# First batch: the tails of q and k are cast by GpSimd, without warming matmuls ahead of their transposes, and one h1 block is evacuated by ScalarE

## The chip, the cores and the metric

The kernel runs on one core of a Trainium2 chip. The time is device microseconds of one execution. Three executions of the kernel before gave 298.59, 298.76 and 299.44 us; the median is 298.76 us. One more execution was recorded by the hardware profiler; all rows of a trace come from that one.

The engines are named as the profile names them: PE is the tensor engine (PEld its weight loads), DVE the vector engine, ACT the scalar engine, POOL is GpSimd, and SP only issues transfers. Each runs its own queue in order and waits on semaphores for the others.

## The reference, cut to what matters

Two layers, one after the other. First an attention over 8 batches, 8 heads, 576 positions and 64 columns a head, in which heads 0 to 3 ("plain") see the last 32 positions and heads 4 to 7 ("dilated") every fourth of the last 128:

```python
scores = scale * np.matmul(q, k.transpose(0, 1, 3, 2))
mask_plain = (rel >= 0) & (rel < 32)
mask_dil = (rel >= 0) & (rel < 128) & (rel % 4 == 0)
attn = softmax(np.where(masks, scores, -1e9))
x = np.matmul(attn, v)            # to (batch, 576, 512): heads beside each other
```

Then a mixer on `x`, first over the positions, then over the columns:

```python
h = np.maximum(xt @ w_tok1, 0.0) @ w_tok2      # 576 -> 256 -> 576, xt is x transposed
u = x + h.transpose(0, 2, 1)
h2 = np.maximum(u @ w_ch1, 0.0) @ w_ch2        # 512 -> 1536 -> 512
return u + h2
```

Inputs and output are float32; the kernel computes in float16 with float32 sums.

## The kernel before, in words

**Tiles.** Positions are worked on in blocks of 128: four full blocks and a tail of 64 (positions 512 to 575). For q and k the 512 main positions of a pair of heads (hp = 0 to 3) lie in `l_q` and `l_k` in float32 and are cast to float16 (`c_q`, `c_k`; `cast_qk`, L252). The tails of q and k of all heads lie together in one tile `lt`, q in partitions 0 to 63 and k in 64 to 127; one cast (`cast_tails_qk`, L258, recorded at the helper's line L103) makes `c_t` of it.

**From cast to scores.** PE transposes the casts into PSUM (`transposes`, L304, tiles `tp_q` and `tp_k`). For the first batch ACT or DVE copies q into `qz` and DVE copies k into `kt` (L315). The tails have a function of their own in the first batch, `first_tails` (L388): four transposes of `c_t` into `tp_t`, and three copies on DVE into `qz` (L398, twice) and `kt` (L399). Scores (`sc` and, for the last blocks, `sm`) are matmuls of `kt` and `qz` (L406) with a masking matmul ahead of each (L404); ACT takes the exponential into `attp` (plain) or `attd` (dilated). `values` (L471) multiplies with v into `av`; DVE forms a reciprocal (L501) and the normalised `xn`.

**The mixer.** `emit_h1` (L504) makes h1 in four pieces: `jb` counts the two blocks of 128 hidden rows, and `half` the two halves of the columns, 0 for the plain heads and 1 for the dilated. Each piece is five matmuls into `h1p` and one relu on its way to SBUF. In the first batch `u_half` (L819) then makes u piece by piece. `w1n` is the first token weight with its rows in natural order; `natural_w1` (L779) builds it on PE from `w1p` and `spread`. `emit_uT` transposes u, and the channel matmuls (`gp`, L645, then `yp`, L664) follow.

**The order.** It is written out by hand: each engine executes its instructions in the order in which the program emits them. The first batch is a straight list (L717 to L850); after it a generator of channel matmuls for batch b is interleaved with steps of the batches behind it, by planned times. POOL's list for the first batch runs L743 to L765: a cast of q, the late memsets (`emit_fixed_late`, L171), then transfers of weights and casts of q, k and v in turn. POOL issues those weight transfers itself, so they stand in the same order as its casts; SP and ACT issue the loads of q, k and v. The second batch's loads start behind two small copies on POOL (`gate`, L732) that wait for weight transfers.

**PSUM.** Three banks called `fl` and three called `main` are taken in turn, and two for scores. `warm` (L708) takes a `main` bank and runs matmuls of zeros (`idle`) into it that nobody reads: eight at the start (L767) and two at L794.

The list of the first batch around the change:

```python
    tp(1)
    cast_tails_qk(0, nc.vector)
    warm(2)
    first_tails()
    ts[7]()
    ts[8]()
    cast_qk(0, "k", 2, nc.vector)
    ts[10]()
```

Here `tp(hp)` is the transposes of q and k of a pair of heads with their copies, and `ts[5 * hp + i]` is step i of that pair: 0 and 1 the transposes of q and k, 2 and 3 the scores of its two heads, 4 the last blocks.

Of the kernel before, what the change touches and what calls it, by code (L numbers as in the profile page):

```python
# [69 lines left out]
def kernel(  # L70
# [11 lines left out]
    nc = tc.nc  # L82
# [9 lines left out]
    def bank(tag, bufs, name, dtype=FP32):  # L92

        if tag in turn:
            turn[tag] += 1
            tag, bufs = f"{tag}{turn[tag] % bufs}", 1
        return ps.tile([128, 512 if dtype == FP32 else 1024], dtype, tag=tag, bufs=bufs, name=name)

    def copy(eng, out, in_):
        if eng is nc.scalar:  # L100
            nc.scalar.copy(out=out, in_=in_)  # L101
        else:
            eng.tensor_copy(out=out, in_=in_)  # L103

    def relu(eng, out, in_):
        if eng is nc.scalar:
            nc.scalar.activation(out=out, in_=in_, func=AF.Relu)  # L107
        else:
            eng.tensor_scalar_max(out=out, in0=in_, scalar1=0.0)  # L109
# [61 lines left out]
    def emit_fixed_late():  # L171
        for i in range(2):
            nc.gpsimd.memset(vv[i][64:128, 4], 0.0)
            nc.gpsimd.memset(vv[i][:, :, :, 64:65], 1.0)
            nc.gpsimd.memset(vt[i][:, :, 64:65], 1.0)
            nc.gpsimd.memset(w1t[i], 0.0)
        nc.gpsimd.memset(w2a[:, :, S:640], 0.0)
# [74 lines left out]
    def cast_qk(b, nm, hp, eng):  # L252
        if (b, nm) not in c16:
            c16[(b, nm)] = sb.tile([128, 4, 4, 2, D], FP16, tag=f"c_{nm}", bufs=1, name=f"c_{nm}_{b}")
        copy(eng, c16[(b, nm)][:, hp],
             l32[(b, nm, hp // 2)][:, 2 * (hp % 2):2 * (hp % 2) + 2].rearrange("m h r d -> m r h d"))

    def cast_tails_qk(b, eng):  # L258
        c16[(b, "t")] = sb.tile([128, H, D], FP16, tag="c_t", bufs=1, name=f"c_t_{b}")
        copy(eng, c16[(b, "t")], l32[(b, "t")])  # L260
# [127 lines left out]
    def first_tails():  # L388

        p = bank("fl", 3, "tp_t", FP16)  # L390
        for hp in range(4):
            nc.tensor.transpose(
                out=p[:, 128 * hp:128 * hp + 128],
                in_=c16[(0, "t")][:, 2 * hp:2 * hp + 2, :].rearrange("m h d -> m (h d)"), identity=ident)
        t = p[:, 0:512].rearrange("p (x n c) -> p x n c", n=2, c=64)
        for h in range(2):
            rows = slice(64 * h, 64 * h + 64)
            nc.vector.tensor_copy(out=qza[rows, :, h, 512:S], in_=t[rows, :, 0])  # L398
        nc.vector.tensor_copy(out=kta[:, :, 512:S], in_=t[:, :, 1])  # L399
# [104 lines left out]
    def emit_h1(b, jb, half, t):  # L504
        x = xn[b]
        j = slice(jb, DTOK, 2)
        c = slice(256 * half, 256 * half + 256)
        w = w1p if half else w1n
        p = bank("fl", 3, f"h1p_{b}_{jb}_{half}")[:, 0:256]
        nc.tensor.matmul(out=p, lhsT=w1t[b % 2][:, j], rhs=x[:, 4, c], start=True, stop=False)  # L510
        for s in range(4):
            nc.tensor.matmul(out=p, lhsT=w[:, s, j], rhs=x[:, s, c], start=False, stop=(s == 3))  # L512
        relu(nc.vector if b <= 1 and jb else nc.scalar, t[:, c], p)

    def emit_u(b, s, h1):
        p = bank("fl", 3, f"up_{b}_{s}")
# [89 lines left out]
    def mix_steps(b, t_h1, t_h1b, t_u, t_uT, du=1.0):  # L606
        h1 = [sb.tile([128, DM], FP16, tag="h1", bufs=4, name=f"h1_{b}_{jb}") for jb in range(2)]
        steps = []
        for half, at in ((0, t_h1), (1, t_h1b)):
            for jb in range(2):  # L610
                steps.append((at + 0.9 * jb, 0.55, lambda jb=jb, half=half: emit_h1(b, jb, half, h1[jb])))
        for i, s in enumerate((4, 0, 1, 2, 3)):
            steps.append((t_u + du * i, 0.44, lambda s=s: emit_u(b, s, h1)))
        if turned(b):
            for t, tail in ((2.0, True), (6.0, False)):
                steps.append((t_u + t * du, 0.0, lambda tail=tail: uT_dma(b, tail)))
            for i, cb in enumerate(CBS):
                steps.append((t_uT + 0.5 * i, 0.0, lambda cb=cb: uT_place(b, cb)))
        else:
            for i, cb in enumerate(CBS):  # L620
                steps.append((t_uT + 0.9 * i, 0.28, lambda cb=cb: emit_uT(b, cb)))
        return steps
# [85 lines left out]
    def warm(n):  # L708

        p = bank("main", 3, "idle_p")  # L710
        for _ in range(n):
            nc.tensor.matmul(out=p, lhsT=idle[:, 0:128], rhs=idle, start=True, stop=True)
# [29 lines left out]
                            op0=ALU.subtract, op1=ALU.mult)  # L742
    cast_qk(0, "q", 1, nc.gpsimd)  # L743
    emit_fixed_late()
    nc.gpsimd.dma_start(out=w1t[0][0:64], in_=moe_w_tok1[512:S, :])
    nc.gpsimd.tensor_copy(out=spread[:, 3:515:4], in_=ident)
    for hp in range(2, 4):
# [23 lines left out]
    def tp(hp):  # L771
        ts[5 * hp]()
        ts[5 * hp + 1]()
# [16 lines left out]
    ts[3]()  # L790
    cast_qk(0, "k", 1, nc.vector)
    tp(1)
    cast_tails_qk(0, nc.vector)
    warm(2)  # L794
    first_tails()
    ts[7]()
    ts[8]()
# [38 lines left out]
    for jb in range(2):  # L836
        emit_h1(0, jb, 0, h1[jb])
    for s in (0, 2):
        u_half(s, 0)
    for jb in range(2):  # L840
        emit_h1(0, jb, 1, h1[jb])
# [101 lines left out]
```

## Time and profile before

| | |
|---|---|
| median of three executions | 298.76 us (298.59 to 299.44) |
| the profiled execution | 298.87 us |
| its span, first to last instruction | 297.1 us |
| PE busy | 283.5 us (95%) |
| PEld busy | 221.4 us |
| DVE busy | 155.6 us |
| ACT busy | 132.1 us |
| POOL busy | 181.6 us |
| PE busy from 6 to 16 us | 6.89 of 10 us |
| PE busy from 16 to 24 us | 6.92 of 8 us |
| PE busy from 29 to 44 us | 14.96 of 15 us |

The span is smaller than the time of the same execution by 1.8 us, which lie around the first and the last instruction. In rows of the trace in order of time, the first number is the start in us, the second the duration; then come engine, line, operation, output and input, their shapes, and how many instructions are put together. A bracket at the end gives the time for which the engine stood idle before, and what it waited for. In the chain of waits a row has the start, the duration and the piece of work. A row of a transfer group ends with the size and the time in us from issue to landing. Matmuls are pipelined, and their recorded durations overlap.

### The profile page before, as it was taken

To read this page: it belongs to the slowest core of one execution; us is meant where nothing else is said; L and a number is where in the kernel's file an instruction comes from. 1 tells how busy PE (TensorE), PEld (TensorE's weight loads), DVE (VectorE), ACT (ScalarE), POOL (GpSimd) and SP (SyncE) were. 2 spreads that over 40 slices of the span, in tenths; PEclk is the share of its full clock that TensorE was granted. 3 is DMA by queue.
4 is the path that set the end of the run, shared out by engine and by line. 5 is a ranking of instruction groups with operands and counts; after the bars stand their busy time and mean duration, and the time that the engine had idled before them with its cause. 6 is when DMAs were issued, how large, how long until landed. Compare 5 with 4: busy or idle time off the path is not lost.

```text
span 297.1 us, 7477 instructions
## 1 busy us (share of the span) xinstructions
PE 283.5 (95%) x3012; PEld 221.4 (75%) x3012; DVE 155.6 (52%) x328; ACT 132.1 (44%) x258; POOL 181.6 (61%) x245
## 2 busy tenths in 40 slices
PE   5698999999999999999999999999999999999994
PEld 2596579986767987688676977697777977796594
DVE  5776338656837966632745155723843265423022
ACT  2763326456652634347444544356345624323400
POOL 7992056428998899839992999459992920000000
PEclk9999999999999999999999999999999999999999
DMA  7999999953999699799679988499955220421023
GB/s 219 269 217 181 211 315 232 330 156 92 327 209 171 188 266 222 160 255 287 170 111 261 240 244 159 104 280 241 189 78 105 77 71 2 86 83 63 2 73 105
DMA packets 104562, 52.36 MB, mean 176 GB/s; under 512 B 72880, under 2 KB 103472, under 8 KB 104528
## 3 DMA queue, kind: packets, MB, share of 16 engines
q1 hardware_dynamic: 100288, 46.81, 65.6%
q0 software_dynamic: 2640, 3.91, 7.4%
q10 hardware_dynamic: 1600, 1.18, 1.3%
q8 instruction: 23, 0.38, 0.5%
q14 instruction: 11, 0.09, 0.1%
HBM read 37.04 MB, written 9.44 MB: 156 GB/s over the span
## 4 chain that ended last, share of the span: by engine, by line
PE 89%; DVE 4%; ACT 2%; DMA 2%; issue 1%; ACTq 0%; POOLq 0%
PE yp L664 27%; PE gp L645 27%; PE sc L406 5%; PE h1p L512 4%; PE gt L636 4%; PE up L524 4%; PE yp L684 4%; DMA const<-consts 2%; PE sm L406 2%; ACT utd L582 1%; PE av L482 1%; PE h1p L510 1%; PE av L493 1%; PE up L535 1%; PE sc L404 1%
## 5 line engine op out<-in xcount | busy, mean ns | idle before, releaser
L664 PE MATMUL yp<-w,gt 128*128 128x256 f16 x756 | 93.2, 273 | 0.7 <-DVE gt L109 0.7
L664 PEld LDWEIGHTS <-gt 128*128 128x128 f16 x768 | 76.5, 106 | 5.5 <-issue 0.9
L107 ACT ACTIVATE gt<-gp 128x512 f16<-128x512 f32 x69 | 41.2, 597 | 71.4 <-PE gp L645 71.1
L645 PEld LDWEIGHTS <-w 128*128 128x128 f16 x384 | 39.2, 114 | 22.7 <-issue 2.1
L113 POOL TENSOR_TENSOR attp<-attp,const 128x1280 f16<-128x1280 f16 (+1 forms) x24 | 36.4, 1543 | 30.2 <-ACT attp L435 30.0
L674 DVE TENSOR_TENSOR o<-yp,u 128x512 f32<-128x512 f32 x31 | 21.3, 690 | 57.6 <-PE yp L664 55.6
L645 PE MATMUL gp<-utd,w 128*128 128x512 f16 x120 | 45.6, 380 | 0.6 <-ACT utd L582 0.4
L645 PE MATMUL gp<-utm,w 128*128 128x512 f16 x120 | 45.5, 379 | 0.0
L645 PE MATMUL gp<-uT,w 128*128 128x512 f16 x144 | 37.3, 379 | 0.2 <-ACT uT L101 0.2
L113 POOL TENSOR_TENSOR attd<-attd,const 128x1024 f16<-128x1024 f16 (+1 forms) x24 | 32.8, 1399 | 0.0
L113 DVE TENSOR_TENSOR xn<-av,rec 128x320 f16<-128x320 f32 x64 | 31.5, 491 | 2.2
L109 DVE TENSOR_SCALAR gt<-gp 128x512 f16<-128x512 f32 x27 | 18.6, 688 | 17.3 <-PE gp L645 16.4
L406 PEld LDWEIGHTS <-kt 128*128 128x128 f16 x272 | 22.4, 101 | 4.1 <-DVE kt L315 1.7
L426 ACT ACTIVATE attp<-sc 128x480 f16<-128x480 f32 x32 | 17.7, 571 | 13.0 <-PE sc L406 12.3
L373 POOL COPY qz<-qt 64x512 f16<-64x512 f16 x20 | 21.5, 1077 | 0.6
L530 DVE TENSOR_TENSOR u<-up,xn 128x512 f16<-128x512 f32 x26 | 17.4, 689 | 8.3 <-PE up L524 8.1
L103 POOL CAST c_q<-l_q 128x512 f16<-128x512 f32 x31 | 19.2, 622 | 3.5 <-DMA l_q<-in_q_dram 3.5
L103 POOL CAST c_k<-l_k 128x512 f16<-128x512 f32 x29 | 17.8, 616 | 5.0 <-DMA l_k<-in_k_dram 4.1
L455 ACT ACTIVATE attd<-sc 128x512 f16<-128x512 f32 x32 | 18.7, 597 | 4.8 <-PE sc L406 4.2
L107 ACT ACTIVATE h<-h1p 128x256 f16<-128x256 f32 x28 | 10.7, 383 | 21.6 <-PE h1p L512 21.6
L406 PE MATMUL sc<-qz,kt 128*128 128x160 f16 (+1 forms) x144 | 18.1, 228 | 1.3 <-DVE kt L315 1.3
L501 DVE RECIPROCAL rec<-av 128x5 f32<-128x5 f32 x64 | 12.2, 190 | 13.6 <-PE av L488 7.0
(139 smaller groups left out, 487.1 us busy)
## 6 DMA issues: line engine op xcount, KB each, us to landing
out_dram<-o SPq DMA_DIRECT2D x72, 128.0 KB, 3.1
l_q<-in_q_dram SPq DMA_DIRECT2D x15, 512.0 KB, 6.3
l_k<-in_k_dram SPq DMA_DIRECT2D x14, 512.0 KB, 5.7
l_vn<-in_v_dram SPq DMA_DIRECT2D x32, 128.0 KB, 6.3
l_vd<-in_v_dram SPq DMA_DIRECT2D x16, 256.0 KB, 4.1
w<-in_moe_w_ch_dram POOLq DMA_DIRECT2D x6, 512.0 KB, 7.6
lt<-in_q_dram SPq DMA_DIRECT2D x8, 128.0 KB, 3.8
l_vt<-in_v_dram SPq DMA_DIRECT2D x8, 128.0 KB, 4.8
```

Of the source, the lines that this page charges most:

```text
L103: eng.tensor_copy(out=out, in_=in_)
L107: nc.scalar.activation(out=out, in_=in_, func=AF.Relu)
L109: eng.tensor_scalar_max(out=out, in0=in_, scalar1=0.0)
L113: eng.tensor_tensor(out=out, in0=x, in1=y, op=ALU.mult)
L373: nc.gpsimd.tensor_copy(out=natural(qz[hp][halves[h], h, 0:512]), in_=qta[halves[h], hp].rearrange("p r m -> p m r"))
L406: nc.tensor.matmul(out=out, lhsT=lhsT, rhs=qz[hp][:, h, queries], start=hide is None, stop=True)
L426: nc.scalar.activation(out=blocks[:, h, 0:3, 0:BLK], in_=p[:, 0:3 * BLK].rearrange("p (b c) -> p b c", c=BLK), func=AF.Exp, scale=0.125)
L455: nc.scalar.activation(out=a[:, h, 0:DTL], in_=p, func=AF.Exp, scale=0.125)
L530: nc.vector.tensor_tensor(out=u16(b, s), in0=blocks4(p), in1=blocks4(xn[b][:, s]), op=ALU.add)
L645: nc.tensor.matmul(out=p, lhsT=w3_block(cb, mb), rhs=uT[(b, cb)][0], start=(i == 0), stop=(i == 3))
L664: nc.tensor.matmul(out=p[:, c], lhsT=gta[:, mb, a0:m0 + 512:4] if half else gta[:, mb, a0:a0 + 128], rhs=w4[mb][:, c], start=(mb == 0), st ...
L674: nc.vector.tensor_tensor(out=blocks4(o32), in0=blocks4(p), in1=u16(b, s), op=ALU.add)
```

## The change

Three edits, all in the first batch. The cast of the tails of q and k is moved from DVE's list to POOL's: it stands behind the late memsets and ahead of the transfer of `w1t`. The two warming matmuls that stood between the second pair's transposes and those of the tails are left out. And the relu of one piece of h1, `jb` = 1 of the plain half, goes from DVE to ACT; in the dilated half of the first batch that of `jb` = 1 stays on DVE, as do both of the second batch.

```diff
-        relu(nc.vector if b <= 1 and jb else nc.scalar, t[:, c], p)
+        relu(nc.vector if jb and (b == 1 or (b == 0 and half)) else nc.scalar, t[:, c], p)
...
     cast_qk(0, "q", 1, nc.gpsimd)
     emit_fixed_late()
+    cast_tails_qk(0, nc.gpsimd)
     nc.gpsimd.dma_start(out=w1t[0][0:64], in_=moe_w_tok1[512:S, :])
     nc.gpsimd.tensor_copy(out=spread[:, 3:515:4], in_=ident)
...
     cast_qk(0, "k", 1, nc.vector)
     tp(1)
-    cast_tails_qk(0, nc.vector)
-    warm(2)
     first_tails()
     ts[7]()
     ts[8]()
```

## The prediction

> **What bounds the kernel now.** I read the page first, then the chain of work that ended last, then the order of time over the first 30 us.
>
> ```profile
> span 297.1 us, 7477 instructions
> PE 283.5 (95%) x3012; PEld 221.4 (75%) x3012; DVE 155.6 (52%) x328; ACT 132.1 (44%) x258; POOL 181.6 (61%) x245
> PE 89%; DVE 4%; ACT 2%; DMA 2%; issue 1%; ACTq 0%; POOLq 0%
> ```
>
> TensorE (PE) is busy 283.5 of 297.1 us and makes 89% of the chain. So time is won only where PE stands still, and the edits lie where it does: the first batch's opening, before the stream of channel matmuls starts at 29 us. The chain there, in order of time:
>
> ```profile
> 10.37 0.75 DVE c_t L103
> 11.17 0.41 PE tp_t L392 x4
> ...
> 14.47 0.70 DVE kt L315
> 15.22 0.25 PE sc L406
> ...
> 23.27 0.34 DVE h L109
> ```
>
> Two pieces of VectorE (DVE) that the change takes away stand on this chain: the cast of the tails (c_t, 10.37) and the evacuation of an h1 block (h, 23.27). Both set PE's pace, so both should be worth something. The question is what is late next.
>
> **First edit: the tails' cast and the warming matmuls.** Around it the engines do this:
>
> ```profile
> 9.56 0.59 PE L712 MATMUL idle_p<-idle 128*128 128x512 f16 x2
> 9.76 0.69 DVE L315 COPY kt<-tp_k 128x512 f16<-128x512 f16 x1 [0.93 <-PE tp_k L310]
> 9.82 1.18 ACT L101 COPY qz<-tp_q 64x512 f16<-64x512 f16 x2
> 10.37 0.74 DVE L103 CAST c_t<-lt 128x512 f16<-128x512 f32 x1
> 11.61 0.61 DVE L398 COPY qz<-tp_t 64x256 f16<-64x256 f16 x2 [0.49 <-PE tp_t L392]
> 12.23 0.39 PE L310 MATMUL tp_q<-const,c_q 128*128 128x128 f16 x4
> 12.45 1.22 DVE L103 CAST c_k<-l_k 128x512 f16<-128x512 f32 x1
> 13.73 0.40 PE L310 MATMUL tp_k<-const,c_k 128*128 128x128 f16 x4 [0.32 <-DVE c_k L103]
> ```
>
> *On GpSimd (POOL).* The cast comes behind the late memsets and in front of everything else that POOL does for this batch:
>
> ```profile
> 1.81 0.71 ACTq L197 DMA_DIRECT2D lt<-in_k_dram  x1
> lt<-in_k_dram ACTq DMA_DIRECT2D x1, 128.0 KB, 6.9
> 8.93 0.54 POOL L745 DMA_DIRECT2D w1t<-in_moe_w_tok_dram  x1
> 10.22 1.36 POOL L103 CAST c_q<-l_q 128x512 f16<-128x512 f32 x2 [0.28 <-DMA l_q<-in_q_dram]
> 11.53 0.56 POOL L749 DMA_DIRECT2D w1p<-in_moe_w_tok_dram  x1
> 12.09 0.62 POOL L103 CAST c_k<-l_k 128x512 f16<-128x512 f32 x1
> ```
>
> The later tail lands at 1.81 + 6.9 = 8.7, and POOL comes to it at 8.93, so the new wait should cost nothing (a landing 0.5 us later would push the whole POOL row by 0.3). The cast has the shape of the one at 12.09 and takes 0.6: c_t is ready at 9.55 instead of 11.11. Queued behind it are the w1t load, the spread copy, two casts of q, the w1p load, a cast of k and the casts of v, all about 0.55 later. But POOL now stands idle 0.28 before 10.22, for a transfer. And its two casts of q take 1.36 for what should be about 1.17 (each next one starts 0.55 behind the one before it at 12.09), while the DVE's c_t runs beside them. Without that c_t the pair shrinks by 0.2. So c_q for heads 4 and 5 is ready at about 11.1 instead of 10.8, and w1p is issued between 11.6 and 12.1 (bounds: all slack taken, or the whole 0.55 shift kept).
>
> *On DVE.* Gone are c_t (0.74) and the 0.49 wait for PE. After the kt copy ends at 10.45, the three tail copies run at 10.45 to 11.25, and the cast of k for heads 4 and 5 can begin at 11.25 instead of 12.45: 1.20 earlier. It took 1.22 here against 0.74 for c_t, of the same shape, with POOL casting at 12.09 to 12.7. In the new place POOL casts q until about 11.65. I take 0.9, ending at 12.15; with the old 1.22 it would be 12.45.
>
> [...]
>
> *On PE.* tp_t can run at about 9.6 and takes 0.4. Then the scores of heads 2 and 3 wait for kt (10.45) and for the two qz copies on ScalarE (ACT; 10.4 and 11.0), and end at 11.45 against 12.23 before. From there PE runs without a stop: from tp_q to tp_k for heads 4 and 5 it took 1.50, of which at least 0.32 was the wait for c_k, so tp_k starts at 12.5 to 12.6 against 13.73 (c_k is ready at 12.15 to 12.45). DVE then copies qz until about 13.0 and kt (0.70) until 13.7, where the chain has kt end at 15.17. So scores for heads 4 and 5 start at about 13.7 instead of 15.22: 1.5 earlier. ACT is next:
>
> ```profile
> 12.02 1.03 ACT L426 ACTIVATE attp<-sc 128x480 f16<-128x480 f32 x2 [1.02 <-PE sc L406]
> 14.39 1.17 ACT L101 COPY qz<-tp_q 64x512 f16<-64x512 f16 x2 [0.23 <-PE tp_q L310]
> 15.84 1.09 ACT L455 ACTIVATE attd<-sc 128x512 f16<-128x512 f32 x2 [0.28 <-PE sc L406]
> ```
>
> Its idle 1.02 goes. Its chain of exponentials and the qz copy of heads 6 and 7 end at about 14.45 instead of 15.56, and the next exponential starts at 14.5 instead of 15.84. The score banks are then free 1.35 earlier, which is what PE keeps of the 1.5.
>
> Two transfers do not move with this:
>
> ```profile
> w1p<-in_moe_w_tok_dram POOLq DMA_DIRECT2D x1, 256.0 KB, 5.5
> 8.74 1.36 SPq L208 DMA_DIRECT2D l_vt<-in_v_dram  x1
> l_vt<-in_v_dram SPq DMA_DIRECT2D x1, 128.0 KB, 5.8
> 18.54 1.91 PE L783 MATMUL w_p<-w1p,spread 128*128 128x256 f16 x16
> ```
>
> l_vt lands at 14.55, just as DVE comes to its cast (about 14.3): no loss. w1p lands at 11.6 + 5.5 = 17.1 to 12.1 + 5.5 = 17.6, and PE comes to its matmuls at 18.54 - 1.35 = 17.2. So they start between 17.2 and 17.6, gaining 0.9 to 1.35; I take **1.2**. The bank counter also makes one step less, as the warming bank is no longer asked for; the tiles that then share a bank are free in time by the rows above (kt copied at 10.45, first small scores read by ACT at 12.9).
>
> Were everything on POOL later by 0.55 and the cast of k blocked for its full 1.22, the first edit would still bring 0.5 or so; its lower bound is 0.4, the upper the 1.5 at the scores.
>
> **Second edit: h1 on ACT.**
>
> ```profile
> 21.67 0.60 PE L512 MATMUL h1p<-xn,w1n 128*128 128x256 f16 x4
> 21.76 0.38 ACT L107 ACTIVATE h<-h1p 128x256 f16<-128x256 f32 x1 [0.69 <-PE h1p L512]
> 22.78 0.49 DVE L113 TENSOR_TENSOR xn<-av,rec 128x320 f16<-128x320 f32 x1
> 23.18 0.41 DVE L109 TENSOR_SCALAR h<-h1p 128x256 f16<-128x256 f32 x1
> 23.65 0.27 PE L829 MATMUL up<-h,w 128*128 128x256 f16 x1 [1.08 <-DVE h L109]
> 24.09 0.27 PE L510 MATMUL h1p<-xn,w1t 128*128 128x256 f16 x1
> ```
>
> The block is summed at 22.27, but DVE works its queue in order and first finishes the values of heads 4 to 7, until 23.27. ACT is idle from 22.14 and can read the bank at 22.3, done at 22.69. The u matmuls then start at 22.75 instead of 23.65: 0.90. They take 0.44, and what follows, the h1 blocks of the dilated half, needs the last xn, at 23.27. So it starts at 23.33 instead of 24.09: **0.76**. That is what is late next, and it moves with the first edit, because the xn row starts when PE delivers the values of head 4. ACT's later work (two u copies, a relu) comes earlier by as much; nothing waits behind the moved 0.38. From 24.09 on PE runs without a visible stop into the channel matmuls.
>
> **Sum.** 1.20 + 0.76 = 1.96. The profiled execution took 298.87, its span 297.1 and 1.8 around it, which does not change; 298.87 - 1.96 = 296.9. It lies 0.11 above the median of 298.76, so I keep 296.9, with 296.4 to 297.6 as this case's own range (1.50 + 0.90, and 0.5 + 0.76).
>
> **Does the later work let it through?** Batch 1's transfers start behind a weight transfer, not behind PE:
>
> ```profile
> 24.96 0.18 POOL L733 COPY w<-w 1x1 f16<-1x1 f16 x1 [3.28 <-DMA w<-in_moe_w_ch_dram]
> 41.10 0.61 POOL L103 CAST c_q<-l_q 128x512 f16<-128x512 f32 x1
> 45.01 0.39 PE L310 MATMUL tp_q<-const,c_q 128*128 128x128 f16 x4
> ```
>
> They stay where they are or slip by up to 0.55, while PE comes 2.0 earlier. The shortest lead among the casts of batch 1 is the one shown: ready at 41.71, used at 45.01, 3.3 us. 2.0 + 0.55 = 2.55 is covered. Later waits on the chain are for ACT and DVE results, which move with PE.
>
> **Rivals.** *Transfers hold the first edit back.* w1p, or the casts queued behind c_t, come later than the bounds above, and PE gains about 0.4 there; 0.76 stays: 298.87 - 1.2 = 297.7. For it speaks that w1p has hardly any lead in the new order; against it, that POOL has 0.28 idle to give.
>
> *Only one edit survives, or batch 1's casts come too late.* Should batch 1's transfers slip by 1.3 us more than reckoned, the 3.3 us lead is gone and PE waits at 43 us for each further tenth. Then 0 to 0.8 is left: 298.1 to 298.9, about 298.4. The lead speaks against it.
>
> *The change does not do what it says:* the tails' cast on POOL is no earlier than on DVE if lt lands after 10.4. The 8.7 above excludes that unless transfers in this stretch scatter by 1.7 us; it falls under the rival before.
>
> *Slower: PE's clock.* The two warming matmuls fill 0.43 of a wait of 1.6 us. The clock shows in the spacing of equal matmuls:
>
> ```profile
> 2.55 3.59 PE L712 MATMUL idle_p<-idle 128*128 128x512 f16 x8 [2.55 <-POOL idle L159]
> ```
>
> Eight of 512 columns take 3.59 us here, 0.43 apart; at 9.56 two take 0.59, 0.22 apart. So PE starts at half pace and is at full pace by 9.5. If leaving out the two drops it back, the array work from 13.7 to 17.0 (3.3 us) runs at half pace and costs 3.3: 298.87 - 1.96 + 3.3 = 300.2. It decides once more than 2 us of array work runs slow. Against it: PE waits 1.18 between 9.99 and 11.17 today and comes out fast (tp_t takes 0.41 in the chain, tp_q in the row at 12.23 0.39), and in the new order tp_t falls into that gap and no wait exceeds 0.7.
>
> [...]
>
> **How the numbers follow.** Forecast 0.65, transfers 0.16, one edit or none 0.13, clock 0.04, and 0.02 for more than 2.4. A difference under 0.3%, 0.9 us, cannot be told from none here, so faster means under 297.86: nearly all of the forecast, two thirds of the transfer case and little of the next, 0.80. Same takes 0.15, slower 0.05. The range runs from 296.2 to 298.1; it leaves out the clock case and most of the case in which one edit or none is left.
>
> **What would show it.** In the changed profile c_t stands on POOL at 8.9 to 9.6 and tp_t on PE before 10; the k cast on DVE starts near 11.3; the w_p matmuls at 17.2 to 17.6, with any wait before them put down to w1p; h on ACT, and the idle 1.08 before the u matmuls gone, with the second h1 pair behind the last xn; channel matmuls from 27.0 instead of 28.9. I am wrong if POOL waits for lt, if w_p starts after 18.1, if PE idles near 42 us for a cast of batch 1, or if equal matmuls after 10 us stand twice as far apart.

## The result, and the profile after

The changed kernel took 296.47 us at the median (295.96 to 296.67, four executions), the kernel before beside it 299.03 us (298.59 to 299.44, four). The ratio is 0.9925, 95% interval 0.9901 to 0.9948: faster, by 0.75%. The forecast was 296.9, with 296.4 to 297.6 as its own range. The profiled execution took 296.67 us against 298.87 before, 2.20 less, where the sum had 1.96. The time agrees with the forecast, but the 2.20 is made of other pieces than the 1.96, and in larger samples the medians lie 1.3 apart rather than 2.56; both are taken apart below.

The page of the changed kernel: its span, the busy time of the engines, and the chain that ended last by engine.

```profile
span 294.9 us, 7473 instructions
...
PE 283.1 (96%) x3010; PEld 221.1 (75%) x3010; DVE 153.7 (52%) x326; ACT 132.5 (45%) x259; POOL 181.5 (62%) x246
...
PE 83%; DMA 6%; POOL 4%; ACT 2%; DVE 2%; SPq 1%; issue 1%; ACTq 0%; POOLq 0%
```

PE is as busy as before (283.1 against 283.5), so what was won is idle time. In the chain PE fell from 89% to 83% and DVE from 4% to 2%; transfers rose from 2% to 6%, and POOL, which had no work of its own on the chain before, has 4%. In this execution POOL and the loads around it bound the opening, where DVE did before.

The first 18 us of the changed kernel in order of time (start, duration, engine, line, operation; the bracket is the idle time before and what ended it):

```profile
6.45 0.61 POOL L103 CAST c_q<-l_q 128x512 f16<-128x512 f32 x1 [1.42 <-DMA l_q<-in_q_dram]
...
9.71 0.62 POOL L103 CAST c_t<-lt 128x512 f16<-128x512 f32 x1
...
10.38 0.40 PE L392 MATMUL tp_t<-const,c_t 128*128 128x128 f16 x4 [0.69 <-POOL c_t L103]
...
11.67 1.08 DVE L103 CAST c_k<-l_k 128x512 f16<-128x512 f32 x1
...
12.19 0.67 POOL L750 DMA_DIRECT2D w1p<-in_moe_w_tok_dram  x1
...
14.29 0.25 PE L406 MATMUL sc<-qz,kt 128*128 128x128 f16 x1 [0.29 <-DVE kt L315]
...
17.61 1.91 PE L784 MATMUL w_p<-w1p,spread 128*128 128x256 f16 x16
```

The tails' cast is on POOL, but at 9.71, not at 8.93. It does not wait for its own input: POOL's whole list is late, since its first cast waited until 6.45 for a block of q. So tp_t starts at 10.38 instead of 9.6, the scores of heads 4 and 5 at 14.29 instead of 13.7, and the w_p matmuls at 17.61, the late end of the predicted 17.2 to 17.6. Against 18.54 before that is 0.93.

The second edit, in the same view:

```profile
21.38 0.38 ACT L107 ACTIVATE h<-h1p 128x256 f16<-128x256 f32 x1 [0.16 <-PE h1p L512]
...
21.82 0.27 PE L828 MATMUL up<-h,w 128*128 128x256 f16 x1 [0.17 <-ACT h L107]
...
21.85 0.49 DVE L113 TENSOR_TENSOR xn<-av,rec 128x320 f16<-128x320 f32 x1
...
22.39 0.27 PE L510 MATMUL h1p<-xn,w1t 128*128 128x256 f16 x1
...
27.88 1.46 PE L645 MATMUL gp<-uT,w 128*128 128x512 f16 x6 [0.28 <-DMA w<-in_moe_w_ch_dram]
```

The relu is on ACT, the idle 1.08 before the u matmuls has become 0.17, and the second pair of h1 blocks starts at 22.39, 0.05 behind the end of the last xn (21.85 + 0.49). From w_p to this pair it is 4.78 us, where it was 24.09 - 18.54 = 5.55. The last row is new: the second matmul of the channel stream now waits 0.28 for a weight transfer. The chain of waits names it: the third of the three loads of channel weights, which POOL requests at 18.46 and which lands 9.28 later, at 27.74. In the kernel before it was requested at 18.14 and landed 9.3 later, at 27.4, before the first gp matmul at 28.91.

Two more pieces lie far behind the opening. First the kernel before, then the changed one, in order of time (rows of PE and ACT around 40 to 52 us):

```profile
41.23 1.04 PE L664 MATMUL yp<-w,gt 128*128 128x256 f16 x8
...
51.29 0.44 ACT L435 ACTIVATE attp<-sm 128x320 f16<-128x320 f32 x1 [0.49 <-PE tp_k L310]
...
51.95 0.22 PE L404 MATMUL sc<-veil,const 128*128 128x128 f16 x1 [0.41 <-ACT attp L438]
...
52.39 0.82 PE L664 MATMUL yp<-w,gt 128*128 128x256 f16 x6
```

```profile
39.62 1.15 PE L664 MATMUL yp<-w,gt 128*128 128x256 f16 x9
...
49.35 0.44 ACT L435 ACTIVATE attp<-sm 128x320 f16<-128x320 f32 x1 [0.16 <-PE sm L406]
...
50.45 0.82 PE L664 MATMUL yp<-w,gt 128*128 128x256 f16 x6
```

At 51.3 us ACT stood idle for 0.49 before an exponential in the kernel before, and PE then waited 0.41 for ACT. In the changed kernel that wait does not occur. PE's lead is 1.61 at the first yp row and 1.94 at the second: 0.33 more. The last row of the chain of waits, before and then after (start, duration, piece of work):

```profile
293.28 0.42 DVE o L672
```

```profile
291.36 0.42 DVE o L672
```

The span runs on for 297.1 - 293.70 = 3.40 behind the last DVE instruction before, and for 294.9 - 291.78 = 3.12 now: another 0.28.

So the 2.20 of the two profiled executions is 0.93 (first edit) + 0.77 (second) - 0.09 (new wait for weights, 1.70 becoming 1.61) + 0.33 (the stall at 51 us) - 0.02 (between there and the end) + 0.28 (the end). The new wait costs less than its 0.28, because PE loses time at this place in the kernel before as well: from the first gp matmul to the first yp it is 12.32 us before and 12.41 after.

### The profile page after: what moved, and what is told of

The parts are those of the page before. It is cut to its first block, busy times and chain, and to the rows that moved or that the text cites. A ratio compares the mean times of both kernels' runs of the same rounds, so it can differ in the third digit from the quotient of the medians.

```text
span 294.9 us, 7473 instructions
## 1 busy us (share of the span) xinstructions
PE 283.1 (96%) x3010; PEld 221.1 (75%) x3010; DVE 153.7 (52%) x326; ACT 132.5 (45%) x259; POOL 181.5 (62%) x246
## 4 chain that ended last, share of the span: by engine, by line
PE 83%; DMA 6%; POOL 4%; ACT 2%; DVE 2%; SPq 1%; issue 1%; ACTq 0%; POOLq 0%
PE gp L645 27%; PE yp L664 26%; PE gt L636 4%; PE h1p L512 4%; PE up L524 4%; PE sc L406 4%; PE yp L684 4%; DMA w<-in_moe_w_ch_dram 3%; DMA l_q<-in_q_dram 2%; ACT utd L582 1%; PE sm L406 1%; PE av L493 1%; PE h1p L510 1%; PE av L482 1%; PE up L535 1%; DMA l_vt<-in_v_dram 1%
```

## The experiments

The edits are shown against the changed kernel. Times are medians with the lowest and the highest execution, and each stands beside executions of the kernel before on the same chip.

### The parts alone, and again

*The first edit alone* (e1). The h1 block stays on DVE.

```diff
-        relu(nc.vector if jb and (b == 1 or (b == 0 and half)) else nc.scalar, t[:, c], p)
+        relu(nc.vector if b <= 1 and jb else nc.scalar, t[:, c], p)
```

> Only the first edit: the tails cast by GpSimd, no two warming matmuls; the h1 block stays on VectorE. Theory A (the two edits add up, as in the sum): 0.9 to 1.3 us below the kernel before, the w_p matmuls at 17.2 to 17.7, and the wait of about 1.1 us before the u matmuls still there. Rival B (the edits do not add: VectorE's queue at 23 us is what ends the opening, and moving its front earlier is taken back there): within 0.4 us of the kernel before.

297.41 us at the median (297.0 to 298.21, 12 executions) against 298.26 (35 executions): ratio 0.9965 (0.9946 to 0.9984). That is 0.85 at the median, just short of theory A's 0.9 to 1.3 and more than rival B's 0.4. Its opening, in order of time, and the wait for ACT:

```profile
11.34 0.54 DVE L103 CAST c_k<-l_k 128x512 f16<-128x512 f32 x1 [0.32 <-DMA l_k<-in_k_dram]
...
17.17 1.91 PE L784 MATMUL w_p<-w1p,spread 128*128 128x256 f16 x16
...
22.71 0.27 PE L510 MATMUL h1p<-xn,w1t 128*128 128x256 f16 x1
...
50.61 0.22 PE L404 MATMUL sc<-veil,const 128*128 128x128 f16 x1 [0.45 <-ACT attp L438]
```

Here POOL was in time, and w_p starts at 17.17, the early end of the prediction. From w_p to the second h1 pair it is 5.54, as before the change, and the wait of 0.45 for ACT is there as well.

*The second edit alone* (e2, e9). Tails on DVE and warming matmuls as before the change, the h1 block on ACT. It ran twice, with other runs of the kernel before beside it.

```diff
     emit_fixed_late()
-    cast_tails_qk(0, nc.gpsimd)
...
     tp(1)
+    cast_tails_qk(0, nc.vector)
+    warm(2)
     first_tails()
```

> Only the second edit: the h1 block on ScalarE, everything else as before. Theory A: 0.76 us below the kernel before, with the second pair of h1 blocks starting 0.06 us behind the last xn. Rival B (the edit is worth the whole wait): 0.9 to 1.1 us below. Rival C (the gain of the changed kernel is nearly all from the first edit): within 0.3 us.

> Only the second edit, once more, beside the changed kernel in the same call, so that the difference of the two is what the first edit is worth. Theory A (as in the sum): 0.9 to 1.3 us slower than the changed kernel at the median. Rival B (in the usual execution VectorE's casts and GpSimd's do not collide, and the front of the kernel before is already as fast as e2's profile, with the w_p matmuls at 17.5): 0 to 0.4 us slower. In the profile, VectorE's cast of k for heads 4 and 5 takes about 0.6 us where GpSimd is not casting beside it, and 1 us or more where it is.

296.84 (296.5 to 299.03, 12) against 298.26, ratio 0.9956 (0.9934 to 0.9978); the second time 297.32 (296.67 to 299.03, 12) against 298.05 (24), ratio 0.9964 (0.9943 to 0.9985). This edit alone is thus worth between 0.7 and 1.4 at the median, which leaves theory A and rival B of e2 open and excludes rival C. Of its first profile, in order of time:

```profile
10.26 0.42 DVE L103 CAST c_t<-lt 128x512 f16<-128x512 f32 x1
...
10.50 1.21 POOL L103 CAST c_q<-l_q 128x512 f16<-128x512 f32 x2 [0.93 <-DMA l_q<-in_q_dram]
...
12.02 0.62 DVE L103 CAST c_k<-l_k 128x512 f16<-128x512 f32 x1
...
12.22 0.88 POOL L103 CAST c_k<-l_k 128x512 f16<-128x512 f32 x1
...
17.50 1.91 PE L783 MATMUL w_p<-w1p,spread 128*128 128x256 f16 x16
...
22.29 0.27 PE L510 MATMUL h1p<-xn,w1t 128*128 128x256 f16 x1
```

Up to 21 us this kernel has the instructions of the kernel before, yet w_p starts at 17.50 and not at 18.54. The difference lies in two DVE casts: c_t takes 0.42 where it took 0.74, and the cast of k 0.62 where it took 1.22. Here POOL waited 0.93 for a block of q and began 0.24 behind c_t; and the cast of k began ahead of POOL's at 12.22, which then took 0.88 instead of 0.62. In these rows the engine that comes second pays, and which one it is changes from one execution to the next with the landing of a transfer. That is read from these rows and not tested by itself; but the profile on which the prediction was built had caught the opening in which DVE paid twice.

*The changed kernel again* (e5, e11), without an edit, beside the runs that it is compared with.

> The changed kernel as it is, in more executions and beside the kernel before on the same chip. Theory A (two steps that add up: 0.76 for h1, 0.9 to 1.3 for the tails): 1.7 to 2.1 us below the kernel before at the median, with executions in two groups if PE's clock comes up at different times. Rival B (the 2.6 us first seen is the size): 2.4 us or more below.

> The changed kernel once more, as the measure for the two runs beside it. Theory A and its rivals differ here only in what the others do: 296.5 to 296.9, 1.3 to 1.9 us below the kernel before.

296.84 (296.26 to 297.81, 9) against 298.19 (28), ratio 0.9927 (0.9901 to 0.9952); and 296.75 (296.1 to 297.68, 11) against 298.05, ratio 0.9945 (0.9926 to 0.9964). The differences of the medians are 1.35 and 1.30: less than both theories of e5 had, and the low end of what was expected of e11. In the first comparison it had been 2.56, since the four executions of the kernel before there all lay between 298.59 and 299.44, while its medians in larger samples are 298.05 to 298.26.

What does the first edit add to the second? Of both kernels there is a profile with PE at full pace from 7 us on (four transposes in 0.38 at 6.57 and at 6.65): e9 (second edit alone) and e5 (both edits). In order of time, e9 and then e5:

```profile
14.11 0.25 PE L406 MATMUL sc<-qz,kt 128*128 128x128 f16 x1 [0.58 <-DVE kt L315]
...
17.43 1.91 PE L783 MATMUL w_p<-w1p,spread 128*128 128x256 f16 x16
...
27.58 3.65 PE L645 MATMUL gp<-uT,w 128*128 128x512 f16 x16 [0.17 <-DMA w<-in_moe_w_ch_dram]
```

```profile
9.52 0.40 PE L392 MATMUL tp_t<-const,c_t 128*128 128x128 f16 x4
...
11.25 0.69 DVE L103 CAST c_k<-l_k 128x512 f16<-128x512 f32 x1 [0.26 <-DMA l_k<-in_k_dram]
...
13.49 0.25 PE L406 MATMUL sc<-qz,kt 128*128 128x128 f16 x1 [0.19 <-DVE kt L315]
...
14.57 0.47 DVE L103 CAST vv<-l_vt 64x512 f16<-64x512 f32 x1 [0.54 <-DMA l_vt<-in_v_dram]
...
14.80 0.19 PE L486 MATMUL av<-vv,attp 128*128 128x65 f16 x1
15.09 0.19 PE L488 MATMUL av<-vv,attp 128*128 128x65 f16 x1
...
17.04 0.19 PE L488 MATMUL av<-vv,attp 128*128 128x65 f16 x1
...
17.21 1.91 PE L784 MATMUL w_p<-w1p,spread 128*128 128x256 f16 x16
...
27.58 3.62 PE L645 MATMUL gp<-uT,w 128*128 128x512 f16 x16 [0.39 <-DMA w<-in_moe_w_ch_dram]
```

The first edit does bring the scores of heads 4 and 5 forward, from 14.11 to 13.49: 0.62. Then it gives that back three times. The values' matmul of the tail (L488) starts 0.29 behind the one before it, where such matmuls follow each other at 0.03 (15.34 and 15.37 in the same trace), because DVE had to wait for the tail of v: 0.26. Between the last value matmul and w_p lie 0.17 instead of 0.03, since w1p, requested at 11.61, lands only 5.5 later, at about 17.1: 0.14. And the second matmul of the channel stream starts at 27.58 in both kernels, because it waits for the same weights, which land at 27.44 and 27.45: at the first yp matmul, at 39.36 and 39.32, 0.04 is left of the last 0.22. What stays of the first edit is the shorter end of the span (below), 3.13 against 3.40. The medians agree in size: both edits against the second alone are 296.84 against 296.84 and 296.75 against 297.32, 0 to 0.57. Theory A of e9, 0.9 to 1.3, is out; rival B's 0 to 0.4 is nearer.

So what an edit is worth depends on the other. An estimate from the rows shows it for one opening, that of e9. The kernel before would come to its first yp matmul there at 17.43 + (41.23 - 18.54) = 40.12. The first edit alone comes to it at 39.86 (e1), the second alone at 39.36 (e9), both at 39.32 (e5). That is 0.26, 0.76 and 0.80. With the end of the span (0.28, first edit) and the stall at 51 us (0.33, second) it makes 0.54, 1.09 and 1.41, beside 0.85, 0.73 to 1.42 and 1.30 to 1.35 at the medians. The first edit alone is 0.3 better than these rows explain; the medians of the kernel before hold late openings too, such as that of its profile.

### The warming matmuls and the place of the cast

*The two warming matmuls put back* (e3) into the changed kernel (they multiply zeros).

```diff
     tp(1)
+    warm(2)
     first_tails()
```

> The changed kernel with the two warming matmuls put back between the second pair's transposes and those of the tails. Theory A (PE waits for c_t there anyway): within 0.3 us of the changed kernel, about 296.5. Rival B (PE is ready for the tails when c_t is, so 0.43 us of zeros push the scores): 0.2 to 0.45 us slower than the changed kernel. Rival C (they keep the clock up): faster than the changed kernel, with equal matmuls after 10 us closer together.

297.05 (296.31 to 298.0, 12) against 298.26, ratio 0.9945 (0.9926 to 0.9965). Its profile, in order of time:

```profile
9.65 0.59 PE L712 MATMUL idle_p<-idle 128*128 128x512 f16 x2
...
10.09 0.39 PE L392 MATMUL tp_t<-const,c_t 128*128 128x128 f16 x4
```

The transposes of the tails queue behind the zeros and start at 10.09 instead of e5's 9.52; 0.34 of this comes from c_t, which started at 9.20 here and at 8.86 in e5. In time the two cannot be told apart (297.05 and 296.84), so theory A and rival B stay open; rival C is out. The warming gained nothing that its removal would lose: in e5 PE keeps its pace without the two, with 0.40 for tp_t against 0.39 with them.

*The cast on DVE* (e4), without the warming matmuls and with the h1 block on ACT.

```diff
     emit_fixed_late()
-    cast_tails_qk(0, nc.gpsimd)
...
     tp(1)
+    cast_tails_qk(0, nc.vector)
     first_tails()
```

> The changed kernel with the cast of the tails back on VectorE, behind the copy of kt, still without the two warming matmuls. Theory A (the place of the cast is what the first edit is worth): c_t at 11.1, tp_t at 11.17, and 0.9 to 1.3 us slower than the changed kernel, so about 297.5. Rival B (GpSimd's list, which then is free of the cast, was the bound, and the warming matmuls were the cost): within 0.4 us of the changed kernel.

297.18 (296.61 to 300.64, 12), ratio 0.9981 (0.9948 to 1.0014): at the median 0.34 above the changed kernel, within rival B's 0.4 and short of theory A's 0.9 to 1.3, but with four of twelve executions between 299.18 and 300.64. None of these four was profiled; the profiled execution took 298.22. One cause of long executions is to be seen in the next rows, first of e4, then of the third profile of the changed kernel (e11), in order of time; whether it is the cause of the four is not shown:

```profile
10.15 0.63 PE L310 MATMUL tp_q<-const,c_q 128*128 128x128 f16 x4
...
12.29 0.40 PE L392 MATMUL tp_t<-const,c_t 128*128 128x128 f16 x4 [1.12 <-DVE c_t L103]
```

```profile
2.55 3.59 PE L712 MATMUL idle_p<-idle 128*128 128x512 f16 x8 [2.55 <-POOL idle L159]
...
9.80 0.63 PE L310 MATMUL tp_q<-const,c_q 128*128 128x128 f16 x4
...
10.66 0.63 PE L392 MATMUL tp_t<-const,c_t 128*128 128x128 f16 x4
...
18.07 1.91 PE L784 MATMUL w_p<-w1p,spread 128*128 128x256 f16 x16
```

Four transposes take 0.63 there, and 0.40 in e5 at the same place. In e4, e10 and e11 PE was at half pace until about 11 us, although the same eight start matmuls had run. In e11 that puts w_p at 18.07 instead of e5's 17.21, and the execution took 296.99 instead of 296.43.

*Without the eight start matmuls* (e6), *and with eleven* (e7; zeros again).

```diff
-    warm(8)
```

```diff
-    warm(8)
+    warm(11)
```

> The changed kernel without the eight matmuls of zeros at its start; they are no part of the result. It prices the clock rival: the profile should show matmuls at half pace (160 columns 0.13 us apart, not 0.07) until past 11 us. Theory A (the executions that are 1.2 to 1.5 us longer than the rest are those in which the clock comes up late): 1 to 2.5 us slower than the changed kernel, in all executions. Rival B (PE waits for others in this stretch, so its pace does not matter): within 0.3 us of it.

> The changed kernel with eleven matmuls of zeros at its start instead of eight, so that PE is busy from 2.5 to about 7.2 us rather than 6.0. Theory A (late clock makes the slow group): fewer executions in the slow group, the lowest time up to 0.4 us higher, since the first transposes then start up to 0.4 later. Rival B (the slow group comes from transfers): as many slow executions as the changed kernel, and slower by 0.3 us on the whole.

Without them 298.03 (297.11 to 298.8, 12), ratio 0.9974 (0.9953 to 0.9995), 1.2 above the changed kernel's 296.84; PE was still at half pace at 10.72 (0.63 for the four transposes of the tails), and w_p started at 18.56. With eleven 296.86 (296.38 to 297.88, 8), ratio 0.9927 (0.9901 to 0.9954): no difference. The start matmuls are worth about 1.2, and three more of them nothing that shows at the median. Whether three more make long executions rarer cannot be told from eight. Nor is the 1.2 all shown to be PE's pace, since e11 with the same late pace had w_p at 18.07. The profiled execution with eleven took 297.88 though, for another reason; its waits after 29 us (us in all, times, longest):

```profile
PE tp_k L310 <- POOL c_k L103: 0.6, 1, 0.6
...
PE tp_q L310 <- POOL c_q L103: 0.2, 1, 0.2
```

These two stand at 43.70 and 44.26 us (0.57 and 0.16 in the order of time), in batch 1: the rival that the casts of batch 1 come too late. It occurred in this one profile and in none of the others.

### The order behind the tails

*The tail copies behind the scores* (e8), so that DVE casts k first.

```diff
     tp(1)
-    first_tails()
     ts[7]()
     ts[8]()
     cast_qk(0, "k", 2, nc.vector)
+    first_tails()
     ts[10]()
```

> The changed kernel with the four transposes of the tails and their copies moved behind the scores of heads 2 and 3 and behind the cast of k for heads 4 and 5. Theory A (where c_t comes late on GpSimd, at 10.3 us in the changed kernel's profile, PE's queue stands behind the tails' transposes): the scores of heads 2 and 3 start at 10.5 whatever GpSimd does, and 0.2 to 0.6 us is gained. Rival B (VectorE's own queue sets the pace, as kt for heads 4 and 5 ends the wait): within 0.2 us, or slower, as the tail copies then delay the copies of q.

297.89 (296.57 to 298.97, 12), ratio 0.9975 (0.9952 to 0.9998): 1.05 slower than the changed kernel beside it, as rival B had it. In order of time:

```profile
11.32 1.62 DVE L103 CAST c_k<-l_k 128x512 f16<-128x512 f32 x1 [1.28 <-DMA l_k<-in_k_dram]
...
13.18 0.23 PE L406 MATMUL sm<-qz,kt 128*128 128x160 f16 x1 [1.01 <-DVE qz L398]
```

The cast of k waited 1.28 for its transfer, then took 1.62 beside POOL's casts, and the tail copies, queued behind it, kept PE waiting 1.01. DVE's queue still sets PE's pace when something late stands at its head.

*The second and third piece of the channel weights requested earlier* (e10), to remove the new wait at 27.6 us.

```diff
     load_w3(0)
+    load_w3(1)
+    load_w3(2)
     cast_vd(0, 0, nc.gpsimd)
     cast_vd(0, 2, nc.gpsimd)
-    load_w3(1)
     cast_vx(0, nc.gpsimd)
-    load_w3(2)
```

> The changed kernel with the second and third loads of the channel weights (w3) issued right behind the first, ahead of the casts of v on GpSimd. Theory A (the third load's landing at about 27.5 holds the second channel matmul): the wait of 0.3 to 0.4 us on that transfer is gone, the first gt matmuls come 0.2 us earlier counted from the first gp, and the time falls by 0.1 to 0.3 us. Rival B (the wait is shown there, but the transposes of u end it at the same time): no change. Rival C (the casts of v, now later by 1.5 us, hold the values of head 4): slower by 0.3 us or more, with PE waiting for vv or vt near 19 us.

296.62 (296.08 to 297.45, 8), ratio 0.9947 (0.9929 to 0.9966), against 296.75 for the changed kernel beside it: not to be told apart. Both profiled executions had PE at half pace until about 11 us, so both reached the channel matmuls at 27.67, when the weights were there in any case. But the landing of the third load can be read: requested at 16.30 in e10 it took 11.2 us and landed at about 27.5, while in e5, requested at 17.85, it took 9.6 and landed at 27.45. The earlier request did not bring it earlier, so it would hardly have removed the wait of e5. What holds the load back is not shown.

### The stall at 51 us

It stood in the two profiles with the h1 block on DVE (before, e1) and in none of the eleven with it on ACT. Either the relu's time on ACT matters, or only ACT's place in its own list of instructions. So one more ACT instruction of one element was put into the kernel with the first edit alone, its result read by nobody:

```diff
-        relu(nc.vector if jb and (b == 1 or (b == 0 and half)) else nc.scalar, t[:, c], p)
+        relu(nc.vector if b <= 1 and jb else nc.scalar, t[:, c], p)
...
     natural_w1(0)
+    nc.scalar.activation(out=spark, in_=idle[0:1, 0:1], func=AF.Exp)
     natural_w1(1)
```

> The first edit alone (as e1) with one more instruction of one element on ScalarE between the two copies of w1n. Both kernels with the h1 block on VectorE show a wait of 0.4 us on PE near 50 us, behind ScalarE, which stands idle 0.5 before an exponential whose input is there; the eight others do not. Theory A (it hangs on ScalarE's place in its instruction stream, one instruction more or less): the wait is gone. Rival B (it hangs on what VectorE or PE do): the wait of 0.4 is still there.

One execution (e12), 297.77 us. Its opening was late, with w_p at 18.10: POOL waited for q until 10.97, and so requested w1p only at 12.36. In order of time:

```profile
50.51 0.44 ACT L435 ACTIVATE attp<-sm 128x320 f16<-128x320 f32 x1 [0.16 <-PE sm L406]
```

The wait for ACT is gone although the relu is on DVE. That points to ACT's list being one instruction longer, and not to what the instruction does. The late opening is a weak rival, as the stall stood in openings on both sides of it (w_p at 17.17 in e1, at 18.54 before). It rests on one profile, and by which mechanism is not shown.

## Why the prediction was right, and where it was not

**What bounds the kernel, and that both edits act on it:** right. Idle time of PE in the opening went, and nothing else had to.

**The cast on POOL costs no wait, "ready at 9.55":** right for the input, which had landed at 8.8 when POOL came to it at 9.71, and in e5 c_t was on POOL at 8.86; in e3 and e6 the cast did wait for its input, 0.20 and 0.32. In the changed kernel's first profile it came at 9.71, because an earlier cast in POOL's queue waited 1.42 for q where it had waited 0.61 before. I took POOL's list of one execution for a fixed one.

**DVE's cast of k, "I take 0.9":** mis-sized by the overlap, as its two ends said. It took 1.08 in the changed kernel, 0.69 in e5, 0.54 in e1; 1.62 in e8. It began 0.58, 0.42, 0.26 and 0.88 before POOL's two casts of q ended: in these four, the longer POOL casts beside it, the longer it takes. In e12 it was the other way round: the cast of k began 0.89 before the end of POOL's two and took 0.43, and POOL's two took 1.44 instead of 1.17 to 1.19. The mechanism is not shown. Nor is it shown whether such a cast holds up the issue of w1p beside it: that took 0.67 at 12.19 beside the cast of 1.08, but 0.56, as before the change, at 12.14 beside the cast of 1.62 in e8. w1p was requested just behind the late bound in the changed kernel's first profile, because POOL's whole list was late, and at 11.61, the early bound, in e5.

**First edit 1.20:** the step that failed. Its pieces came as forecast: scores of heads 4 and 5 at 13.49 in e5 (13.7 forecast), w_p at 17.21 (17.2 to 17.6). But they were subtracted from an opening that was itself about 1.0 later than in two other profiles: the kernel with these same instructions started w_p at 17.50 and 17.43 in e2 and e9, not at 18.54. Against that opening the edit wins 0.22 at w_p, and 0.04 is left of it at the first yp matmul when the second edit is there too. At the medians it is worth 0.85 alone and 0 to 0.57 beside the second edit, not 1.20. The rows that would have warned were at hand: c_t took 0.74 and the cast of k 1.22, and the casts of k at 4.79 and 8.20 in the same profile, of the same shape, only 0.53 and 0.63. I wrote of what POOL would gain once c_t is gone from beside its casts, and did not ask how often the two meet. "l_vt lands at 14.55: no loss" failed as well: DVE stood there 0.54, and PE lost 0.26. "w1p has hardly any lead" was right, and cost 0.14. So the rival that transfers hold the first edit back was nearer to this step than the forecast; it named w1p and POOL's casts, and missed the tail of v and the channel weights.

**Second edit 0.76:** right to a hundredth. From w_p to the second h1 pair it is 5.55, 5.54 and 5.55 with the block on DVE (before, e1, e12), and 4.78, 4.79, 4.78 and 4.78 on ACT (after, e2, e5, e9), and the pair starts behind the last xn as the prediction said.

**"From 24.09 on PE runs without a visible stop into the channel matmuls":** this held for the order, not for the weights. With both edits PE arrives before a weight transfer and waits 0.28 in the first profile of the changed kernel, 0.39 in e5. The net loss is smaller: from the first gp matmul to the first yp it is 12.32 us before, 12.41 and 12.51 in these two, so 0.09 and 0.19.

**"Later waits on the chain move with PE":** one did not. The stall of 0.33 at 51 us went with the second edit, which is therefore worth about 1.1 by the rows (0.76 + 0.33). That, and the 0.28 at the end, made up for the first edit, so that the sum came out near where it was forecast, for two reasons that were not in it. This is luck. The time of 296.9 held in the larger samples too (296.84 and 296.75); the gain of 1.96 did not (1.35 and 1.30), because the 298.87 from which it was subtracted was a long execution of the kernel before.

**The clock:** right that leaving out the two warming matmuls does not lower PE's pace: four transposes take 0.40 in e5 without them, 0.39 in e3 with them. The sign that was named for it, equal matmuls twice as far apart after 10 us, did appear in e4, e10 and e11, but for another reason: PE was at half pace there before it came to the place of the two (tp_q at 9.80 takes 0.63 in e11). What was not seen is that PE's pace comes up at different times in executions of one kernel, and e11, with the late pace, took 0.56 longer than e5.

**The lead of batch 1's casts, 3.3 us:** enough in every profile but that with eleven start matmuls, where PE waited 0.7 for them; it is the sign "if PE idles near 42 us", in one profile.

No kernel here is clearly faster than the changed one: e10 at 296.62 and the changed kernel at 296.75 beside it overlap.

## What to carry to other kernels

A gain read from one profiled execution is a gain against that execution's accidents: before a wait is priced, see whether the durations around it are what the same shapes take elsewhere in the trace, and take the dear ones for chance until shown otherwise. Where an edit brings PE forward, list every transfer that does not move with it up to the next long stretch of matmuls, down to leads of a few tenths; here three of them took back nearly all of 0.62 us one after the other. The edit that shortens a fixed chain (a block read by an idle engine instead of a queued one) came out at its predicted size in every run, the one that depends on who casts when did not.

## What the runs showed of the hardware

- **PE's pace after the same warming.** The eight start matmuls end between 5.8 and 6.2 us in every profile that has them. In e5 four transposes take 0.38 at 6.65; in e11 they take 0.63 still at 10.66. Between 7 and 11 us the same kernel runs in one or the other way. The granted clock in the profile is 9 tenths or more in every slice of both; only the spacing of the matmuls shows it (those of 160 columns stand 0.07 apart in e5 from 8.12 on, 0.13 in e11 from 8.61 on). Full pace at 6.65 and half pace still at 10.66 lie 4.0 us apart in two executions of one kernel. PE stands idle between pieces of work in both (0.51 before 6.65 in e5, 0.43 before 6.57 in e11); what decides the moment is not shown.
- **The landing of a load that does not follow its request.** The third load of channel weights landed at about 27.5 us in e10, requested at 16.30, and at 27.45 in e5, requested at 17.85. The cause is not shown.
- **A wait that goes with the number of instructions.** With one ACT instruction more, at 19.65 us (e12, one profile) or as the relu at 21 us (eleven profiles), ACT's idle time near 50 us is 0.33 shorter (0.16 against 0.49). What ACT does in it is not in the trace.
- **The end of the span.** Behind the last DVE instruction the span runs on for 3.36 to 3.40 us in the four profiles of kernels that cast the tails on DVE (before, e2, e4, e9) and for 3.01 to 3.13 in the ten that cast them on POOL. No cause was tested; the two groups do not overlap.
